# Batch 0 of a fused attention and gated feed-forward kernel: half of k by another queue, six rows per partition, and another unit shape in the first stage

## The chip, the cores and the metric

The kernel runs on one core of one Trainium2 chip. The metric is the device time of one execution in microseconds, as the median of several runs. One execution is also taken with the hardware profiler; its times are those of that one execution. "Span" is the time from its first to its last instruction.

## The reference

Inputs are q, k, v of shape (8 batches, 8 heads, 576 tokens, 64), float32, and two weights, w_in (512 x 2048) and w_out (2048 x 512).

```python
theta = np.pi / 2.0 * pos / S                 # pos = 0..575, S = 576
phi(x) = concat([relu(x) * cos(theta), relu(x) * sin(theta)])     # 64 -> 128 features
kv  = einsum('bhsf,bhsd->bhfd', phi(k), v);   z = phi(k).sum(axis=s)
num = einsum('bhsf,bhfd->bhsd', phi(q), kv);  den = phi(q) . z + 1e-6
x   = (num / den) as (4608 tokens, 512)       # 512 = 8 heads x 64
h   = x @ w_in;   g = h * cos(h);   out = g @ w_out      # (4608, 512) float32
```

Sums over tokens do not depend on the order of the tokens, so the kernel may spread the tokens over the partitions as it likes, as long as the cosine and sine table and the stores follow.

## The kernel before

**Stages.** The 4608 tokens are nine chunks of 512 (`CH`). For each chunk there is a first product M1 (x times w_in), then cosine and product, then a second product M2 (g times w_out). Attention for the eight batches of 576 tokens is woven between these products. Every engine works through its instructions in the order in which the program emits them: `plan` and `at(chunk, step, function, ...)` list what is emitted after which step, and `run(c, s)` emits it. Nothing reorders it afterwards.

**The start, batch 0.** While the inputs travel, TensorE runs products of zeros (`warm`, 33 of them). q is stored with six consecutive tokens on each of 96 partitions (`R = 6`, `PR = 96`); k and v with five consecutive tokens on 112 partitions and four on four more (`RK = 5`, `PK = 116`), so each needs a second small load (`load_rest`). All these loads are issued by GpSimd's queue, which turns float32 into float16 on the way. The queue of SyncE only brings the table `CS`, the identity `ID` and some zeros. `scaled` makes phi: for one token index i it emits two instructions (t = 0 for cosine, t = 1 for sine), each a relu and a product with a column of `CS`. VectorE does most of them; five for k and both for q's i = 4 go to ScalarE. `q_turn` transposes phi(q) of one i on TensorE (eight small products into `QT`), and ScalarE copies `QT` into `X`. `kv_head` sums phi(k) times v over i (five products for each head); ScalarE copies the sums into `kvz`. `num_tile` makes one tile of 128 tokens of the numerators and denominators on TensorE (`NP`) and divides on VectorE (`dn`, `rd`, `x`). `x_turn` transposes it on TensorE (`XP`), and ScalarE, or VectorE for tile 1, copies it into `XT`, from which M1 reads. Tile 0 needs i = 0 and 1, tile 1 needs i = 1 and 2, tile 2 needs i = 2 and 3, and tiles 3 and 4 need i = 4 and 5.

**Chunk 0's M1.** `m1_pair(u, n0, n1)` is a unit: two blocks of 128 columns of w_in by 256 tokens, eight products of 256 columns. Then ScalarE makes the cosine (`co`) and VectorE the product (`g`). Units 0 to 7 go over tiles 0 and 1, units 8 to 15 over tiles 2 and 3. The result of a unit lies in PSUM under the tag `m1` or `m2` by turns, two buffers each, so unit u needs the buffer that unit u-4 has left. `m2_part(0, 0, 0)`, the first of M2, takes such a buffer too. w_in arrives in four groups of four blocks.

**The queue of GpSimd** holds, in this order: k heads 0 to 3, k's rest, k heads 4 to 7, q's i = 0 to 3, v heads 0 and 1, v's rest, v heads 2 to 7 in three loads, w_in group 0, q's i = 4 and 5, w_in groups 1 to 3, w_out groups 0 and 1, then batch 1.

Of the kernel before, what the change touches and what calls it, by code (L numbers as in the profile page):

```python
# [11 lines left out]
ALU = mybir.AluOpType  # L12
# [5 lines left out]
def kernel(  # L18
# [54 lines left out]
    KB = [cpool.tile([PK, H * RUNK], F16, name=f"k{n}") for n in "ab"]  # L73
    VB = [cpool.tile([PK, H * RUNK + D], F16, name=f"v{n}") for n in "ab"]
    ID = cpool.tile([P, P], F16, name="ID")
    WU = cpool.tile([P, CH], F16, name="WU")
    WS = cpool.tile([P, 1], F32, name="WS")
# [14 lines left out]
            q16=lpool.tile([PR, H * RUN], F16, name="q16", tag=f"q16{odd}"),  # L92
        )

    def rows_of(tile_):
        return tile_[:, 0:H * RUNK].rearrange("p (h r) -> p h r", h=H)

    def load_q(b, i0=0, i1=R):
        dst = st[b]["q16"].rearrange("p (h r) -> p h r", h=H)
# [4 lines left out]

    def load_kv(b, which, h0=0, h1=H):
        src = dict(k=k, v=v)[which]
        full = src[b][:, 0:FULL * RK, :].rearrange("h (p i) d -> p h (i d)", i=RK)
        nc.gpsimd.dma_start(  # L108
            out=rows_of(st[b][which + "16"])[0:FULL, h0:h1], in_=full[:, h0:h1],
        )  # L110
# [15 lines left out]

    def scaled(b, which, i, h0=0, h1=H):
        s = st[b]
        rows, n, o = (PR, R, 0) if which == "q" else (PK, RK, R)
        if which + "p" not in s:  # L130
            s[which + "p"] = apool.tile([rows, n, H * F], F16, name=which + "p",
                                        tag=which + "p", bufs=1)
        dst = s[which + "p"][:, i].rearrange("p (h t d) -> p h t d", t=2, d=D)
        src = s[which + "16"][:, 0:H * n * D].rearrange("p (h i d) -> p h i d", i=n, d=D)
        cs = CS[0:rows, :, o + i:o + i + 1]
        for t in range(2):
            if b == 0 and (which == "k" and h0 == 4 and t == 1 or which == "q" and i == 4):
                nc.scalar.activation(
                    out=dst[:, h0:h1, t, :], in_=src[:, h0:h1, i, :], func=AF.Relu,
                    scale=cs[:, t],  # L140
                )
                continue
            nc.vector.tensor_scalar(  # L143
                out=dst[:, h0:h1, t, :], in0=src[:, h0:h1, i, :],
                scalar1=0.0, scalar2=cs[:, t],
                op0=ALU.max, op1=ALU.mult,
            )
# [52 lines left out]
    def kv_head(b, h):  # L200
        s = st[b]
        if h == 0 or (b == 0 and h == 4):
            s["KV"] = psA.tile([P, H, P], F32, name="KV", tag="att")
        if h == 0:
            s["kvz"] = apool.tile([P, H, D + 1], F16, name="kvz", tag="kvz")
        n = P if b == 0 else D + 1
        for i in range(RK):
            if b > 0:
                nc.tensor.matmul(  # L209
                    s["KV"][:, h, 0:n], lhsT=s["kp"][:, i, h * F:(h + 1) * F],  # L210
                    rhs=s["vz"][:, h, i, 0:n], start=(i == 0), stop=(i == RK - 1),
                )
                continue
            base = s["v16"][:, h * RUNK + i * D: h * RUNK + (i + 1) * D]
            vz = bass.AP(
                tensor=base.tensor, offset=base.offset,
                ap=[list(base.ap[0]), [H * RUNK - h * RUNK - i * D, 2], [1, D]],
            )
            nc.tensor.matmul(  # L219
                s["KV"][:, h], lhsT=s["kp"][:, i, h * F:(h + 1) * F], rhs=vz,  # L220
                start=(i == 0), stop=(i == RK - 1),
            )
# [60 lines left out]
    def g_for(c):  # L283
        if ("g", c) not in st:
            st["g", c] = gpool.tile([P, NJT, CH], F16, name="g", tag="g")
        return st["g", c]

    def m1_pair(u, n0, n1):
        j0 = 2 * (u % (NJT // 2))
        M1 = psM.tile([P, 2, CH // 2], F32, name="M1", tag=("m1", "m2")[u % 2])  # L290
        step = P if u == 0 else n1 - n0
        for n in range(n0, n1, step):
            for a in range(2):
                for i in range(NCT):
                    nc.tensor.matmul(  # L295
                        M1[:, a, n - n0:n - n0 + step],
                        lhsT=w_in_sb[:, i, (j0 + a) * P:(j0 + a + 1) * P],
                        rhs=XT[:, i, n:n + step], start=(i == 0), stop=(i == NCT - 1),
                    )
            if u == 0 and n == n0:  # L300
                num_tile(0, 2)
        co = opool.tile([P, 2, CH // 2], F32, name="co", tag="co")
        nc.scalar.activation(out=co, in_=M1, func=AF.Sin, bias=PIH, scale=1.0)  # L303
        nc.vector.tensor_tensor(  # L304
            out=g_for(0)[:, j0:j0 + 2, n0:n1], in0=M1, in1=co, op=ALU.mult,
        )

    def m1_group(c, j):
# [59 lines left out]
    def at(c, s, f, *args):  # L368
        plan.setdefault((c, s), []).append((f, args))
# [10 lines left out]
                load_rest(b, w)  # L380

    def plan_stage0():
        at(0, 0, q_turn, 0, 4)
        at(0, 1, scaled, 0, "q", 5)
        at(0, 1, x_turn, 0, 2)
        at(0, 2, loads, 2, "kvq")
        at(0, 3, q_turn, 0, 5)
        at(0, 4, num_tile, 0, 3)
        at(0, 6, x_turn, 0, 3)
        at(0, 11, num_tile, 0, 4)  # L390
        at(0, 14, x_turn, 0, 4)
# [24 lines left out]
        for i, n in enumerate((-1, 1, 2, 4, 6, 8)):  # L416
            at(0 if n < 0 else 1, z + 15 if n < 0 else n, scaled, 2, "q", i)
            at(0 if n < 0 else 1, z + 15 if n < 0 else n, q_turn, 2, i)
        at(1, 9, loads, 3)
        for h in range(H):  # L420
            at(1, 5 + h // 4, kv_head, 2, h)
# [32 lines left out]
            f(*args)  # L454

    with tc.manual_schedule():
        nc.sync.dma_start(out=CS, in_=cs_dr.ap())
        for n, bufs in enumerate((KB[:1] + VB[:1], KB[1:] + VB[1:])):
            if n:
                nc.sync.dma_start(out=ID, in_=id_dr.ap())  # L460
            for t_ in bufs:
                nc.sync.dma_start(
                    out=rows_of(t_)[FULL:PK, :, REST * D:], in_=zero_dr.ap())
# [3 lines left out]
        tiles_for(0)  # L467
        load_kv(0, "k", 0, 4)
        load_rest(0, "k")
        load_kv(0, "k", 4, 8)  # L470
        load_q(0, 0, 4)
        for h in range(0, H, 2):
            if h == 2:
                load_rest(0, "v")
            load_kv(0, "v", h, h + 2)
        nc.gpsimd.memset(st[0]["v16"][:, H * RUNK:], 1.0)
        load_w_in(0)
        load_q(0, 4, R)
        for g in range(1, 4):
            load_w_in(g)  # L480
        load_w_out(0)
        load_w_out(1)
        loads(1, "kvq")
# [5 lines left out]
            for _ in range(n):  # L489
                nc.tensor.matmul(W, lhsT=WU[:, 0:P], rhs=WU, start=True, stop=True)  # L490

        warm(33)
        for h0 in (0, 4):
            for i in range(RK):
                scaled(0, "k", i, h0, h0 + 4)
        for i in range(4):
            scaled(0, "q", i)
            if i < 2:
                q_turn(0, i)
        for h in range(8):  # L500
            kv_head(0, h)
        q_turn(0, 2, "m2")
        num_tile(0, 0)
# [57 lines left out]
```

## Time and profile before

| what | value |
|---|---|
| median of 3 runs (lowest, highest) | 299.69 us (298.92, 300.45) |
| the profiled execution: its own time | 298.35 us |
| the profiled execution: span | 296.5 us |
| TensorE busy / VectorE / ScalarE / GpSimd | 289.6 / 189.0 / 156.3 / 39.8 us |
| first product of M1 starts (from the span's start) | 18.38 us |
| first product of M2 starts | 35.50 us |
| GpSimd's queue / SyncE's and ScalarE's: bytes | 18.36 MB / 20.08 MB |

The engines are written PE (TensorE), PEld (its weight loads), DVE (VectorE), ACT (ScalarE), POOL (GpSimd) and SP (SyncE). Bytes of a load are counted as they are written, so a float32 input that is turned into float16 counts half of what is read. A line of the timeline has the start, the length, the engine, the line of the program, the operation, what it writes and reads, the shapes, how many instructions were merged, and in brackets the idle time before them with what ended it.

### The profile page before, as it was taken

Reading aid. Unit: us, or ns where it says so; the run is one execution under the profiler, and the core shown is the slowest. Engines: PE = TensorE matmul, PEld = TensorE weight load, DVE = VectorE, ACT = ScalarE, POOL = GpSimd, SP = SyncE. Lnnn points to the kernel's source line nnn. Section 1 sums busy time; section 2 is a strip of 40 time slices with the busy share of each in tenths; the row PEclk is TensorE's granted clock in tenths of the full one; section 3 lists DMA queues with packets and bytes.
Section 4 is the critical chain, followed back from the end, with each engine's and each line's share of the span. In section 5 each row is a group of like instructions: output and inputs, shape, how many; then the busy total and the mean of one; then the engine's idle time right before and its main releaser. Section 6 shows DMA issues by size and latency. Waiting matters only on the chain.

```text
span 296.5 us, 5459 instructions
## 1 busy us (share of the span) xinstructions
PE 289.6 (98%) x2055; PEld 151.7 (51%) x2055; DVE 189.0 (64%) x452; ACT 156.3 (53%) x246; POOL 39.8 (13%) x65
## 2 busy tenths in 40 slices
PE   8899999999999999999999999999999999999994
PEld 3577866554544544455445544554455444444443
DVE  1767888987399666866686768677766267008600
ACT  2587763675357534862477158715771178128511
POOL 8743320005013002100210022000000000000000
PEclk9999999999999999999999999999999999999999
DMA  6999999779999996999799879996802510121022
GB/s 88 182 202 206 199 206 203 182 109 141 172 159 168 159 200 128 196 150 114 130 181 176 149 125 164 149 174 134 167 13 66 123 35 0 38 71 35 2 71 71
DMA packets 78178, 38.83 MB, mean 131 GB/s; under 512 B 48328, under 2 KB 73672, under 8 KB 78152
## 3 DMA queue, kind: packets, MB, share of 16 engines
q0 software_dynamic: 28240, 18.36, 44.7%
q1 hardware_dynamic: 49800, 20.08, 39.8%
q8 instruction: 16, 0.26, 0.4%
q14 instruction: 10, 0.08, 0.1%
q10 hardware_dynamic: 112, 0.05, 0.1%
HBM read 36.76 MB, written 9.44 MB: 156 GB/s over the span
## 4 chain that ended last, share of the span: by engine, by line
PE 92%; DMA 3%; DVE 1%; ACT 1%; POOL 1%; issue 1%; ACTq 0%; POOLq 0%
PE M L342 41%; PE M L311 37%; PE NP L235 4%; PE M L295 3%; PE KV L209 3%; DMA q<-in_q_dram 3%; PE QT L167 1%; PE M L358 1%; PE XP L273 1%; PE KV L219 1%; ACT co L303 1%; DVE qp L143 1%; POOL ka L108 1%; DVE g L304 0%; PE W L490 0%
## 5 line engine op out<-in xcount | busy, mean ns | idle before, releaser
L342 PE MATMUL M<-w_out_sb,g 128*128 128x512 f16 x560 | 128.8, 379 | 0.0
L320 DVE TENSOR_TENSOR g<-M,co 128x512 f16<-128x512 f32 x128 | 87.1, 690 | 54.7 <-ACT co L317 54.7
L311 PE MATMUL M<-XT,w_in_sb 128*128 128x512 f16 x512 | 113.9, 379 | 0.0
L317 ACT ACTIVATE co<-M,PIH 128x512 f32<-128x512 f32 x128 | 88.0, 688 | 26.4 <-PE M L311 26.1
L342 PEld LDWEIGHTS <-g 128*128 128x128 f16 x560 | 52.2, 98 | 56.4
L311 PEld LDWEIGHTS <-w_in_sb 128*128 128x128 f16 x512 | 49.2, 98 | 57.4
L349 ACT ACTIVATE ost<-M 128x512 f32<-128x512 f32 x35 | 20.9, 598 | 90.9 <-PE M L342 76.4
L255 DVE TENSOR_TENSOR x<-NP,rd 128x512 f16<-128x512 f32 x40 | 27.7, 691 | 5.0 <-DMA XT<-x 3.6
L143 DVE TENSOR_SCALAR qp<-q,CS 96x512 f16<-96x512 f16 x94 | 28.5, 350 | 2.4 <-DMA X<-qp 1.4
L143 DVE TENSOR_SCALAR kp<-ka,CS 116x512 f16<-116x512 f16 (+1 forms) x75 | 21.8, 349 | 5.4 <-DMA ka<-in_k_dram 5.4
L235 PEld LDWEIGHTS <-X 128*128 128x128 f16 x320 | 15.3, 98 | 9.3 <-issue 1.2
L100 POOL DMA_DIRECT2D q<-in_q_dram x9 | 7.0, 780 | 90.8 <-DVE qp L143 88.6
L235 PE MATMUL NP<-kvz,X 128*128 128x65 f16 x320 | 17.0, 194 | 0.5 <-issue 0.5
L242 DVE TENSOR_SCALAR dn<-NP 128x8 f32<-128x8 f32 x40 | 6.5, 163 | 15.5 <-PE NP L235 15.1
L295 PE MATMUL M<-XT,w_in_sb 128*128 128x256 f16 (+1 forms) x136 | 15.5, 266 | 0.0
L196 ACT ACTIVATE vz<-va 116x640 f16<-116x640 f16 x20 | 13.5, 728 | 0.0
L304 DVE TENSOR_TENSOR g<-M,co 128x512 f16<-128x512 f32 x16 | 10.8, 688 | 3.6 <-ACT co L303 3.5
L295 PEld LDWEIGHTS <-w_in_sb 128*128 128x128 f16 x136 | 12.3, 98 | 1.3
L303 ACT ACTIVATE co<-M,PIH 128x512 f32<-128x512 f32 x16 | 11.0, 688 | 3.3 <-PE M L295 2.9
L490 PE MATMUL W<-WU 128*128 128x512 f16 x39 | 11.5, 452 | 1.2 <-DVE PIH L465 1.2
L209 PEld LDWEIGHTS <-kp 116*128 116x128 f16 x280 | 10.8, 97 | 3.1
L209 PE MATMUL KV<-vz,kp 116*128 116x65 f16 x280 | 11.3, 193 | 0.0
(42 smaller groups left out, 106.0 us busy)
## 6 DMA issues: line engine op xcount, KB each, us to landing
out_dram<-ost SPq DMA_DIRECT2D x23, 192.0 KB, 2.4
q<-in_q_dram POOLq DMA_DIRECT2D x7, 576.0 KB, 7.5
ka<-in_k_dram POOLq DMA_DIRECT2D x6, 560.0 KB, 14.8
va<-in_v_dram POOLq DMA_DIRECT2D x6, 560.0 KB, 12.1
out_dram<-ost SPq DMA_DIRECT2D x24, 128.0 KB, 5.8
w_in_sb<-in_moe_w_in_dram POOLq DMA_DIRECT2D x4, 512.0 KB, 10.1
w_out_sb<-in_moe_w_out_dram POOLq DMA_DIRECT2D x4, 512.0 KB, 16.5
out_dram<-ost SPq DMA_DIRECT2D x23, 64.0 KB, 2.5
```

The lines of the kernel that those rows point to most:

```text
L143: nc.vector.tensor_scalar(out=dst[:, h0:h1, t, :], in0=src[:, h0:h1, i, :], scalar1=0.0, scalar2=cs[:, t], op0=ALU.max, op1=ALU.mult,)
L196: nc.scalar.activation(out=dst, in_=src[:, h:h + 2], func=AF.Copy)
L209: nc.tensor.matmul(s["KV"][:, h, 0:n], lhsT=s["kp"][:, i, h * F:(h + 1) * F], rhs=s["vz"][:, h, i, 0:n], start=(i == 0), stop=(i == RK - 1),)
L235: nc.tensor.matmul(NP[:, h // 4, o:o + D + 1], lhsT=s["X"][:, h, c0:c0 + P], rhs=s["kvz"][:, h], start=True, stop=True,)
L255: nc.vector.tensor_tensor(out=x4[:, a0:a1], in0=np4[:, a0:a1, :, 0:D], in1=rd[:, a0:a1].broadcast_to((P, a1 - a0, 4, D)), op=ALU.mult,)
L295: nc.tensor.matmul(M1[:, a, n - n0:n - n0 + step], lhsT=w_in_sb[:, i, (j0 + a) * P:(j0 + a + 1) * P], rhs=XT[:, i, n:n + step], start=(i = ...
L303: nc.scalar.activation(out=co, in_=M1, func=AF.Sin, bias=PIH, scale=1.0)
L311: nc.tensor.matmul(M1, lhsT=w_in_sb[:, i, j * P:(j + 1) * P], rhs=XT[:, i, c * CH:(c + 1) * CH], start=(i == 0), stop=(i == NCT - 1),)
L317: nc.scalar.activation(out=co, in_=M1, func=AF.Sin, bias=PIH, scale=1.0,)
L320: nc.vector.tensor_tensor(out=g_for(c)[:, j], in0=M1, in1=co, op=ALU.mult,)
L342: nc.tensor.matmul(M2, lhsT=st["g", c][:, j, m * P:(m + 1) * P], rhs=w_out_sb[:, j], start=(j == 0), stop=(j == NJT - 1),)
L349: nc.scalar.activation(out=ost, in_=M2, func=AF.Copy)
```

## The change

Five things change, all in batch 0 and chunk 0.

1. **k and v of batch 0** lie on 96 partitions with six tokens each, like q. The two rest loads go; `kv_head` sums over six products of 96 rows for each head instead of five of 116.
2. **k heads 0 to 3** are loaded as float32 into a tile `k32` by SyncE's queue, as its first load. `CS` and `ID` go to ScalarE's queue. GpSimd's queue starts with k heads 4 to 7.
3. **`scaled` for k**: 24 instructions instead of 20. ScalarE has the sine of all six i of heads 0 to 3 and of i = 0 to 2 of heads 4 to 7; VectorE has the other 15. For q's i = 4 both go to VectorE, for i = 5 the sine to ScalarE.
4. **Order on TensorE at the start**: 29 products of zeros instead of 33; `q_turn` 0 and 1 stand before heads 0 and 2 of `kv_head`.
5. **Units**: `m1_unit(u, j0, nj, t0)`. Four pairs over tiles 0 and 1, then two units of four blocks by the 128 tokens of tile 2, then four pairs, two units of tile 2, and four units of tile 3. q's i = 4 and 5 are loaded behind w_in group 1, and the steps at which their scaling and turning, tiles 3 and 4 and their turns are emitted change.

```diff
 def load_kv(b, which, h0=0, h1=H):
+    if b == 0:
+        nc.gpsimd.dma_start(
+            out=rows_of(st[b][which + "16"], RUN)[0:PR, h0:h1],
+            in_=src[b].rearrange("h (p i) d -> p h (i d)", i=R)[:, h0:h1],
+        )
+        return
...
 def scaled(b, which, i, h0=0, h1=H):
+        if b == 0 and which == "k" and h0 == 0:
+            src = s["k32"].rearrange("p (h i d) -> p h i d", i=n, d=D)
...
-            if b == 0 and (which == "k" and h0 == 4 and t == 1 or which == "q" and i == 4):
+            if b == 0 and t == 1 and (
+                    which == "k" and (h0 == 0 or i < 3) or which == "q" and i == 5):
                 nc.scalar.activation(
...
 def kv_head(b, h):
-        for i in range(RK):
+        for i in range(RK if b > 0 else R):
...
-    def m1_pair(u, n0, n1):
-        j0 = 2 * (u % (NJT // 2))
-        M1 = psM.tile([P, 2, CH // 2], F32, name="M1", tag=("m1", "m2")[u % 2])
-        step = P if u == 0 else n1 - n0
+    def m1_unit(u, j0, nj, t0):
+        nt = 4 // nj
+        n0 = t0 * P
+        M1 = psM.tile([P, nj, nt * P], F32, name="M1", tag=("m1", "m2")[u % 2])
+        step = P if u == 0 else nt * P
...
     def plan_stage0():
-        at(0, 0, q_turn, 0, 4)
-        at(0, 1, scaled, 0, "q", 5)
         at(0, 1, x_turn, 0, 2)
         at(0, 2, loads, 2, "kvq")
-        at(0, 3, q_turn, 0, 5)
-        at(0, 4, num_tile, 0, 3)
-        at(0, 6, x_turn, 0, 3)
-        at(0, 11, num_tile, 0, 4)
-        at(0, 14, x_turn, 0, 4)
+        at(0, 3, scaled, 0, "q", 4)
+        at(0, 4, q_turn, 0, 4)
+        at(0, 4, scaled, 0, "q", 5)
+        at(0, 5, q_turn, 0, 5)
+        at(0, 7, num_tile, 0, 3)
+        at(0, 10, x_turn, 0, 3)
+        at(0, 12, num_tile, 0, 4)
+        at(0, 15, x_turn, 0, 4)
...
-        nc.sync.dma_start(out=CS, in_=cs_dr.ap())
...
+        st[0]["k32"] = gpool.tile([PR, H // 2 * RUN], F32, name="k32", tag="g")
+        nc.sync.dma_start(
+            out=st[0]["k32"].rearrange("p (h r) -> p h r", r=RUN),
+            in_=k[0].rearrange("h (p i) d -> p h (i d)", i=R)[:, 0:H // 2],
+        )
+        nc.scalar.dma_start(out=CS, in_=cs_dr.ap())
+        nc.scalar.dma_start(out=ID, in_=id_dr.ap())
...
-        load_kv(0, "k", 0, 4)
-        load_rest(0, "k")
         load_kv(0, "k", 4, 8)
         load_q(0, 0, 4)
         for h in range(0, H, 2):
-            if h == 2:
-                load_rest(0, "v")
             load_kv(0, "v", h, h + 2)
...
         load_w_in(0)
+        load_w_in(1)
         load_q(0, 4, R)
...
-        warm(33)
+        warm(29)
...
         for i in range(4):
             scaled(0, "q", i)
-            if i < 2:
-                q_turn(0, i)
         for h in range(8):
+            if h in (0, 2):
+                q_turn(0, h // 2)
             kv_head(0, h)
...
-        scaled(0, "q", 4)
         x_turn(0, 1)
-        for s in range(NJT):
-            n = s // (NJT // 2) * (CH // 2)
-            m1_pair(s, n, n + CH // 2)
+        units = [(2 * p, 2, 0) for p in range(4)] + [(0, 4, 2), (4, 4, 2)]
+        units += [(2 * p, 2, 0) for p in range(4, 8)] + [(8, 4, 2), (12, 4, 2)]
+        units += [(4 * g, 4, 3) for g in range(4)]
+        for s, (j0, nj, t0) in enumerate(units):
+            m1_unit(s, j0, nj, t0)
             run(0, s)
```

More of the change, by code (lines that the diff above doesn't have):

```diff
@@ L72 @@
     CS = cpool.tile([PK, 2, R + RK], F32, name="CS")
-    KB = [cpool.tile([PK, H * RUNK], F16, name=f"k{n}") for n in "ab"]
-    VB = [cpool.tile([PK, H * RUNK + D], F16, name=f"v{n}") for n in "ab"]
+    KB = [cpool.tile([PK, H * w], F16, name=f"k{n}") for n, w in (("a", RUN), ("b", RUNK))]
+    VB = [cpool.tile([PK, H * w + D], F16, name=f"v{n}") for n, w in (("a", RUN), ("b", RUNK))]
     ID = cpool.tile([P, P], F16, name="ID")
@@ L93, in tiles_for, with rows_of @@
         )
-    def rows_of(tile_):
-        return tile_[:, 0:H * RUNK].rearrange("p (h r) -> p h r", h=H)
+    def rows_of(tile_, run=RUNK):
+        return tile_[:, 0:H * run].rearrange("p (h r) -> p h r", h=H)
     def load_q(b, i0=0, i1=R):
@@ L128, in scaled @@
         s = st[b]
-        rows, n, o = (PR, R, 0) if which == "q" else (PK, RK, R)
+        rows, n, o = (PR, R, 0) if which == "q" or b == 0 else (PK, RK, R)
         if which + "p" not in s:
-            s[which + "p"] = apool.tile([rows, n, H * F], F16, name=which + "p",
+            s[which + "p"] = apool.tile([PR if which == "q" else PK, R, H * F], F16, name=which + "p",
                                         tag=which + "p", bufs=1)
-        dst = s[which + "p"][:, i].rearrange("p (h t d) -> p h t d", t=2, d=D)
-        src = s[which + "16"][:, 0:H * n * D].rearrange("p (h i d) -> p h i d", i=n, d=D)
+        dst = s[which + "p"][0:rows, i].rearrange("p (h t d) -> p h t d", t=2, d=D)
+        if b == 0 and which == "k" and h0 == 0:
+            src = s["k32"].rearrange("p (h i d) -> p h i d", i=n, d=D)
+        else:
+            src = s[which + "16"][0:rows, 0:H * n * D].rearrange(
+                "p (h i d) -> p h i d", i=n, d=D)
         cs = CS[0:rows, :, o + i:o + i + 1]
         for t in range(2):
-            if b == 0 and (which == "k" and h0 == 4 and t == 1 or which == "q" and i == 4):
+            if b == 0 and t == 1 and (
+                    which == "k" and (h0 == 0 or i < 3) or which == "q" and i == 5):
                 nc.scalar.activation(
@@ L213, in kv_head @@
                 continue
-            base = s["v16"][:, h * RUNK + i * D: h * RUNK + (i + 1) * D]
+            base = s["v16"][0:PR, h * RUN + i * D: h * RUN + (i + 1) * D]
             vz = bass.AP(
                 tensor=base.tensor, offset=base.offset,
-                ap=[list(base.ap[0]), [H * RUNK - h * RUNK - i * D, 2], [1, D]],
+                ap=[list(base.ap[0]), [H * RUN - h * RUN - i * D, 2], [1, D]],
             )
             nc.tensor.matmul(
-                s["KV"][:, h], lhsT=s["kp"][:, i, h * F:(h + 1) * F], rhs=vz,
-                start=(i == 0), stop=(i == RK - 1),
+                s["KV"][:, h], lhsT=s["kp"][0:PR, i, h * F:(h + 1) * F], rhs=vz,
+                start=(i == 0), stop=(i == R - 1),
             )
@@ L286, in g_for @@
         return st["g", c]
-    def m1_pair(u, n0, n1):
-        j0 = 2 * (u % (NJT // 2))
-        M1 = psM.tile([P, 2, CH // 2], F32, name="M1", tag=("m1", "m2")[u % 2])
-        step = P if u == 0 else n1 - n0
-        for n in range(n0, n1, step):
-            for a in range(2):
+    def m1_unit(u, j0, nj, t0):
[3 more added lines that the diff above has]
+        step = P if u == 0 else nt * P
+        for n in range(0, nt * P, step):
+            for a in range(nj):
                 for i in range(NCT):
                     nc.tensor.matmul(
-                        M1[:, a, n - n0:n - n0 + step],
+                        M1[:, a, n:n + step],
                         lhsT=w_in_sb[:, i, (j0 + a) * P:(j0 + a + 1) * P],
-                        rhs=XT[:, i, n:n + step], start=(i == 0), stop=(i == NCT - 1),
+                        rhs=XT[:, i, n0 + n:n0 + n + step],
+                        start=(i == 0), stop=(i == NCT - 1),
                     )
-            if u == 0 and n == n0:
+            if u == 0 and n == 0:
                 num_tile(0, 2)
-        co = opool.tile([P, 2, CH // 2], F32, name="co", tag="co")
+        co = opool.tile([P, nj, nt * P], F32, name="co", tag="co")
         nc.scalar.activation(out=co, in_=M1, func=AF.Sin, bias=PIH, scale=1.0)
         nc.vector.tensor_tensor(
-            out=g_for(0)[:, j0:j0 + 2, n0:n1], in0=M1, in1=co, op=ALU.mult,
+            out=g_for(0)[:, j0:j0 + nj, n0:n0 + nt * P], in0=M1, in1=co, op=ALU.mult,
         )
@@ L456 @@
     with tc.manual_schedule():
-        nc.sync.dma_start(out=CS, in_=cs_dr.ap())
[L458 to L463, printed above, removed]
+        tiles_for(0)
+        st[0]["k32"] = gpool.tile([PR, H // 2 * RUN], F32, name="k32", tag="g")
[5 more added lines that the diff above has]
+        nc.scalar.dma_start(out=ID, in_=id_dr.ap())
+        for t_ in KB + VB:
+            nc.sync.dma_start(
+                out=rows_of(t_)[FULL:PK, :, REST * D:], in_=zero_dr.ap())
         nc.vector.memset(WU, 0.0)
@@ L466 @@
         nc.scalar.activation(out=WS, in_=PIH, func=AF.Sin)
-        tiles_for(0)
-        load_kv(0, "k", 0, 4)
-        load_rest(0, "k")
         load_kv(0, "k", 4, 8)
@@ L472 @@
         for h in range(0, H, 2):
-            if h == 2:
-                load_rest(0, "v")
             load_kv(0, "v", h, h + 2)
-        nc.gpsimd.memset(st[0]["v16"][:, H * RUNK:], 1.0)
+        nc.gpsimd.memset(st[0]["v16"][0:PR, H * RUN:], 1.0)
         load_w_in(0)
+        load_w_in(1)
         load_q(0, 4, R)
-        for g in range(1, 4):
-            load_w_in(g)
+        load_w_in(2)
+        load_w_in(3)
         load_w_out(0)
@@ L490, in warm @@
                 nc.tensor.matmul(W, lhsT=WU[:, 0:P], rhs=WU, start=True, stop=True)
-        warm(33)
+        warm(29)
         for h0 in (0, 4):
-            for i in range(RK):
+            for i in range(R):
                 scaled(0, "k", i, h0, h0 + 4)
```

## The prediction

> **What bounds the kernel now.** I read the page's busy times and chain first, then the chain in order of time, the DMA issues, the stretches of half a microsecond, and the timeline of the first 37 us.
>
> ```profile
> PE 289.6 (98%) x2055; PEld 151.7 (51%) x2055; DVE 189.0 (64%) x452; ACT 156.3 (53%) x246; POOL 39.8 (13%) x65
> PEclk9999999999999999999999999999999999999999
> PE 92%; DMA 3%; DVE 1%; ACT 1%; POOL 1%; issue 1%; ACTq 0%; POOLq 0%
> ```
>
> PE carries the end: 92% of the chain. Behind the first M1 product (18.38 us) it hardly rests, so what moves PE's first M2 product moves the end one for one. Two quantities decide: when M1 starts, and how long PE needs from there to M2 (35.50, so 17.12 us).
>
> ```profile
> 3.46 7.46 DMA q<-in_q_dram
> 10.92 0.02 issue
> 10.94 1.38 DVE qp L143 x4
> ...
> 12.88 2.23 PE KV L219 x40
> 15.12 0.34 PE QT L167 x8
> ```
>
> The chain in time says what sets the start: q lands at 10.92, DVE scales it, PE turns it, sums KV, turns i = 2, and a fixed string of ACT, DVE and PE steps leads from there to M1.
>
> ```profile
> ka<-in_k_dram POOLq DMA_DIRECT2D x2, 280.0 KB, 5.3
> ...
> q<-in_q_dram POOLq DMA_DIRECT2D x1, 384.0 KB, 7.5
> ...
> ID<-id_const SPq DMA_DIRECT2D x1, 32.0 KB, 4.0
> ```
>
> These are loads, KB as written and us from issue to landing. The stretches show who moves bytes when (last column GB/s):
>
> ```profile
> 1.50:2.00 0.50, 0.50 (x2) 0.15 (x1) 0.00 (x0) 0.50 (x1) 0.50 (x1) 1.00 0.15 18
> 2.00:2.50 0.50, 0.50 (x3) 0.20 (x2) 0.00 (x0) 0.22 (x2) 0.50 (x2) 1.00 0.02 3
> 2.50:3.00 0.50, 0.50 (x3) 0.22 (x2) 0.00 (x0) 0.00 (x0) 0.50 (x2) 1.00 0.30 33
> 4.00:4.50 0.50, 0.50 (x2) 0.15 (x1) 0.00 (x0) 0.00 (x0) 0.50 (x2) 1.00 1.35 200
> ```
>
> SP's first load, issued at 0.74, moves bytes from about 1.6; POOL's first, issued at 1.31, from about 2.8. From 4 us to q's landing the stretches hold 116 to 200 GB/s, 155 in the mean.
>
> The timeline shows what a scaling of q costs PE when it is emitted late (i = 5):
>
> ```profile
> 20.80 0.39 PE L273 MATMUL XP<-ID,x 128*128 128x128 f16 x4
> 21.00 0.69 ACT L303 ACTIVATE co<-M,PIH 128x512 f32<-128x512 f32 x1
> ...
> 21.73 0.69 DVE L304 TENSOR_TENSOR g<-M,co 128x512 f16<-128x512 f32 x1 [0.59 <-ACT co L303]
> ...
> 22.33 0.60 DVE L143 TENSOR_SCALAR qp<-q,CS 96x512 f16<-96x512 f16 x2
> ...
> 22.99 0.51 PE L167 MATMUL QT<-ID,qp 96*128 96x96 f16 x8
> ...
> 23.56 0.80 ACT L186 ACTIVATE X<-QT 128x768 f16<-128x768 f16 x1
> ```
>
> Unit 1 leaves PE at 20.80. Its cosine runs 0.20 later, its g at +0.93, the two scalings behind that g at +1.53, and the turn starts at +2.19. PE had a turn of x (0.22) and two units (0.87 each) to do meanwhile, and still idled 0.22.
>
> **The start, part by part.** Bytes ahead of q's landing: before 280 + 16 + 280 + 384 = 960 KB in POOL's queue; after 288 (as float16; the same float32 reads) by SP, 288 + 384 by POOL: the same 960. If both queues share the same engines, q gains the time by which SP's first bytes are earlier, 1.2 us, and little for dropping the 16 KB rest: q lands at 9.6. Bounds: SP's half costs POOL's queue nothing, 304 KB less at 155 GB/s, 1.9 us, q at 9.0; or SP's lead is lost, q at 10.8. I take 9.6, since CS's row shows the lead. The Trainium skill says it the same way ("DMA: Bandwidth & Descriptors", section "Issuing engines are not separate DMA queues"): queues of several engines interleave on the same 16, so a second one saves only issue time; strictly by it, with no earlier bytes, q would land at 10.8 and the sum below would be 1.2 us more; the trace's earlier SP bytes speak for a part between.
>
> DVE must be through k by 9.6. k's half in SP's queue: 0.74 + 5.3 (POOL's row) less 0.5 for the faster first byte, so about 5.4; the bounds are 4.6 (bytes from 1.6, 288 KB at 200 GB/s, and the 1.6 us by which q's landing trails the stretch in which 960 KB are through) and 6.5 (first rival). Six scalings from float32: no row has that source; the float16 row (15 in 3.38) gives 0.225 each and is one end, the float32 rate of L255 and L242 (0.69 for 512 elements, 0.16 for 8, so 0.42 for 256) the other; 0.30 taken, nearer the same operation: 7.2. The second half of k lands about 1.2 us ahead of the 8.4 at which ACT could start on it, at 7.2; nine scalings at 0.225 end at 9.3. ACT has nine in place of five (five in 2.10, 0.42 each): 5.4 + 2.5, then 1.3: 9.2. Both are just covered by q's 9.6; each us beyond costs a us. CS and ID cost ACT two issues (0.34 and 0.45 on SP) while it has nothing due; CS had moved within 1.3 us of its issue and is wanted at 5.4: nothing. The zero loads, now behind k's half, serve batches 1 and 2 only: nothing.
>
> From q: turn 0 starts 0.67 later as before (10.94 to 11.61); turn 0.34, twelve KV products at 0.056 (40 in 2.23) 0.67, turn 0.34, thirty-six more 2.01: turn 2 at q + 4.03. Before it was 14.95 - 10.94 = 4.01: the eight extra products (0.45) take the place of PE's waits for i = 1. v's last load trails q by its 576 KB as before and is needed 3.4 us after q: covered by 0.2. The zeros end four products (0.86 us) earlier, at 9.9, ahead of turn 0 at 10.3: nothing. From turn 2 to M1 nothing changes, and w_in group 0 (landed by 17.10, where a POOL load had waited for it) comes 1.3 us earlier too, ahead of M1. So M1 starts 1.3 us earlier: **-1.3**, between -1.9 and about 0.
>
> **M1 to M2, walked from M1's first product at 0.** PE's work: a pair is 8 x 0.109 (40 in 4.37) = 0.874; a unit of four blocks is 16 x 0.0558 = 0.893, as the unit in steps of 128 has shown; a turn of q 0.345, of x 0.22, an NP 0.26. Before, 16.14 of work and 0.98 idle make 17.12. After, eight units at +0.019 give 16.29. The idle time:
> - XP2: x2 is ready at 2.09, PE at 2.03: 0.07. (Turn 4 stood there before.)
> - Turn 4: its two scalings now stand behind unit 3's g, and only unit 4 lies between. Unit 3 ends at 4.06; the turn can start 2.19 later, 6.25; PE is through unit 4 at 4.96: **1.30**.
> - Turn 5: ACT's sine for i = 5 is emitted behind turn 4's copy X, which starts 0.57 after the turn, at 6.82; ACT is free 0.69 later and needs 0.71: 8.27. PE has turn 4 until 6.60 and unit 5 until 7.49: **0.78**.
> - Unit 12 reads tile 3: unit 10 ends at 13.26, co10 runs from 13.46, XT3 behind it from 14.04 for 0.60, so 14.72; PE is through unit 11 at 14.38: 0.34.
> - M2 takes unit 13's buffer; that g stands behind tile 4's three DVE steps: 0.14.
>
> Idle 2.63, stage 18.92: **+1.80**. Tiles 3 and 4's other waits (0.20 and 0.51 before) are covered now: two pairs lie before NP3, three units before XP3. w_in group 1, which had landed by 20.69, comes 1.3 us earlier and no longer behind q's 192 KB; unit 2 wants it at 19.4: covered. q's end lands one w_in (2.5 us) later and 1.3 earlier, about 19.2; DVE wants it at 22.7. If it came after that, turn 4 would wait longer by as much.
>
> **Sum.** -1.3 + 1.8 = +0.5 us: the profiled execution's 298.35 (span 296.5 and 1.85 around it) becomes 298.85. It lies 1.34 below the median, so the median becomes 299.69 + 0.5 = 300.2. A measurement of this kernel can tell about 0.5%, 1.5 us, from no change: the forecast is no change, because a start that is won is given back by two turns of q.
>
> **Rivals.**
> *SP's load comes late (slower).* ID, 32 KB in SP's queue beside POOL's loads, took 4.0 us. With that latency and 1.8 us for its bytes k's half lands at 6.5; six scalings at 0.30 and nine at 0.225 end at 10.3, or 11.1 with 0.42 each. M1 then gains 0.6 or nothing: 300.9 to 301.6; with the lead lost for q too (10.8), 301.4. It decides once k's half lands after 5.8. For it: POOL's own first half took 5.3. Against: SP issues 0.6 us before POOL, on idle engines.
> *PE's clock falls (slower).* PE idles 2.1 of the 4.6 us from unit 3's end to unit 6. The first twelve zeros ran at half speed (0.43 against 0.216) for 5.0 us; one such stretch costs 2.5 us: 302.7. Against it: the clock row is whole throughout and the idle 0.74 us before turn 0 left it so. The Trainium skill ("TensorE: Matmul & The Clock Gate", section "HAM oscillation — how this bites in real kernels") forbids only gaps over about 3.4 us; by it this rival does not happen.
> *The turns do not wait (faster).* If q's scalings reach DVE ahead of g3, the 2.08 us of the two turns go: 298.1. Against it: before, L143's pair ran exactly behind the g that it was emitted after.
>
> **How the numbers follow.** Forecast 0.64: slower by over 0.5% 0.05, faster 0.02, the rest within. Late or lost lead 0.22: 0.15 slower, 0.07 within. Clock 0.06, all slower. No waits 0.08: 0.06 faster, 0.02 within. Together 0.08 faster, 0.66 same, 0.26 slower. The forecast alone spans 299.6 (q at 9.0) to 301.2; the range 298.7 to 302.3 leaves out most of the no-wait case, the clock case and the far end of the late load.
>
> **What would show it.** q's first scaling at 9.6 and M1 at 17.1 (start); turn 4 idle 1.3 behind DVE's qp, turn 5 idle 0.8 behind ACT's qp, unit 12 idle 0.3 behind ACT's XT; M1 to M2 in 18.9. It is wrong if M1 starts later than 17.8 or before 16.4, if PE does not stop at the turns, or if the clock row shows less than 9.

## The result, and the profile after

| what | before | after |
|---|---|---|
| median of 21 runs (lowest, highest) | 298.25 us (297.38, 300.45) | 299.48 us (298.37, 302.85) |
| ratio after / before, 95% interval | | 1.0045 (1.0029 to 1.0060) |
| the profiled execution: time, span | 298.35, 296.5 us | 299.29, 297.5 us |
| q's first scaling starts | 10.94 us | 10.04 us |
| first product of M1 starts | 18.38 us | 17.50 us |
| first product of M2 starts | 35.50 us | 36.40 us |
| from M1's first product to M2's | 17.12 us | 18.90 us |
| from the start of PE's last product to the end of the span | 4.00 us | 4.51 us |

The change makes the kernel slower by a little less than half a per cent. With more runs the median of before came to 298.25, 1.44 below the three runs that the prediction started from; the predicted 300.2 lies 0.7 above the measured 299.48, and its difference of +0.5 us stands against a measured +1.2.

On the page after the change, PE is as busy as before, the row of the granted clock is whole, and PE still carries 93% of the chain:

```profile
PE 289.4 (97%) x2123; PEld 153.0 (51%) x2123; DVE 189.6 (64%) x453; ACT 157.4 (53%) x249; POOL 37.9 (13%) x62
PEclk9999999999999999999999999999999999999999
PE 93%; DMA 3%; DVE 1%; ACT 1%; issue 1%; POOL 0%; ACTq 0%; POOLq 0%
```

The chain of waits over the first 60 us (start, length, what) shows both halves of the change. q is scaled 0.90 earlier than before, and KV now runs as twelve products behind the first turn and thirty-six behind the second. Later two scalings of q (DVE at 23.19, ACT at 25.02) and a copy into XT (ACT at 31.57) stand in the chain. Before, the chain ran through ACT and DVE there too (a scaling of q at 22.42, tile 3's division until 26.88), but PE idled for them only 0.2 to 0.5 us at a time:

```profile
2.12 7.90 DMA q<-in_q_dram
10.04 0.62 DVE qp L154 x2
10.71 0.51 PE QT L178 x8
...
12.23 2.01 PE KV L230 x36
...
23.19 0.53 DVE qp L154 x2
...
25.02 0.72 ACT qp L149
...
31.57 0.60 ACT XT L292
```

The timeline shows the two turns. The bracket is the idle time before an instruction and what ended it: PE's weight loader waits 1.30 us for DVE's scaling of i = 4 and 0.78 us for ACT's sine of i = 5. The scaling starts where g of unit 3 (22.50 + 0.69) releases DVE, and the sine where ACT's copy X has started and ACT is free again:

```profile
22.50 0.69 DVE L317 TENSOR_TENSOR g<-M,co 128x512 f16<-128x512 f32 x1 [0.18 <-ACT co L316]
...
23.76 0.37 PEld L178 LDWEIGHTS <-qp 96*128 96x128 f16 x8 [1.30 <-DVE qp L154]
...
24.31 0.81 ACT L197 ACTIVATE X<-QT 128x768 f16<-128x768 f16 x1 [0.96 <-PE QT L178]
...
25.02 0.71 ACT L149 ACTIVATE qp<-q,CS 96x512 f16<-96x512 f16 x1
...
25.78 0.37 PEld L178 LDWEIGHTS <-qp 96*128 96x128 f16 x8 [0.78 <-ACT qp L149]
```

The loads of the start (KB as written, us from issue to landing):

```profile
k<-in_k_dram SPq DMA_DIRECT2D x1, 576.0 KB, 5.0
q<-in_q_dram POOLq DMA_DIRECT2D x1, 384.0 KB, 7.9
ka<-in_k_dram POOLq DMA_DIRECT2D x1, 288.0 KB, 6.2
```

SP's half of k was issued at 0.74 and landed at about 5.7. The stretches show its bytes early, as the prediction had it (last column GB/s; before, the first two held 18 and 3):

```profile
1.50:2.00 0.50, 0.50 (x2) 0.15 (x1) 0.00 (x0) 0.34 (x1) 0.50 (x1) 1.00 0.51 75
2.00:2.50 0.50, 0.50 (x3) 0.20 (x2) 0.00 (x0) 0.50 (x1) 0.50 (x2) 1.00 0.62 167
```

Between the two profiled executions the end moved by +0.96 us: the start -0.88, the stage from M1 to M2 +1.78, waits between M2 and the last product -0.45, and the time after the last product (here and below counted from its start) +0.51. The prediction has the first two; the last two are new.

### The profile page after: what moved, and what is told of

It is laid out like the page before. It is cut to its first block, busy times and chain, and to the rows that moved or that the text cites. A ratio compares the mean times of both kernels' runs of the same rounds, so it can differ in the third digit from the quotient of the medians.

```text
span 297.5 us, 5599 instructions
## 1 busy us (share of the span) xinstructions
PE 289.4 (97%) x2123; PEld 153.0 (51%) x2123; DVE 189.6 (64%) x453; ACT 157.4 (53%) x249; POOL 37.9 (13%) x62
## 4 chain that ended last, share of the span: by engine, by line
PE 93%; DMA 3%; DVE 1%; ACT 1%; issue 1%; POOL 0%; ACTq 0%; POOLq 0%
PE M L355 41%; PE M L324 37%; PE M L307 4%; PE NP L246 4%; PE KV L220 3%; DMA q<-in_q_dram 3%; PE QT L178 1%; PE M L371 1%; PE KV L230 1%; PE XP L284 1%; DVE x L266 0%; DVE qp L154 0%; ACT co L316 0%; POOL ka L108 0%; ACT qp L149 0%
## 5 line engine op out<-in xcount | busy, mean ns | idle before, releaser
L324 PEld LDWEIGHTS <-w_in_sb 128*128 128x128 f16 x512 | 49.3, 98 | 57.3
L154 DVE TENSOR_SCALAR kp<-ka,CS 116x512 f16<-116x512 f16 (+1 forms) x69 | 20.0, 339 | 0.0
L307 PE MATMUL M<-XT,w_in_sb 128*128 128x128 f16 (+1 forms) x200 | 15.6, 234 | 0.1
L307 PEld LDWEIGHTS <-w_in_sb 128*128 128x128 f16 x200 | 13.6, 98 | 0.9 <-issue 0.3
L317 DVE TENSOR_TENSOR g<-M,co 128x512 f16<-128x512 f32 x16 | 10.8, 688 | 4.7 <-ACT co L316 4.6
L504 PE MATMUL W<-WU 128*128 128x512 f16 x35 | 10.8, 469 | 1.2 <-DVE PIH L483 1.2
```

Source lines behind the costliest of these rows:

```text
L154: nc.vector.tensor_scalar(out=dst[:, h0:h1, t, :], in0=src[:, h0:h1, i, :], scalar1=0.0, scalar2=cs[:, t], op0=ALU.max, op1=ALU.mult,)
L307: nc.tensor.matmul(M1[:, a, n:n + step], lhsT=w_in_sb[:, i, (j0 + a) * P:(j0 + a + 1) * P], rhs=XT[:, i, n0 + n:n0 + n + step], start=(i = ...
L324: nc.tensor.matmul(M1, lhsT=w_in_sb[:, i, j * P:(j + 1) * P], rhs=XT[:, i, c * CH:(c + 1) * CH], start=(i == 0), stop=(i == NCT - 1),)
```

## The experiments

Every profile is one execution, and the executions of one kernel differ: the four with the old start (before, the stage alone, and two below) have M1 at 18.38, 18.16, 18.64 and 19.11. So I use the times of twelve executions as well as the profiles, and for M1, the stage and the end the means over the profiles of one kind. Ratios are to the kernel before on the same chip.

### The scalings of q two units earlier

```diff
-        at(0, 3, scaled, 0, "q", 4)
-        at(0, 4, scaled, 0, "q", 5)
+        at(0, 1, scaled, 0, "q", 4)
+        at(0, 2, scaled, 0, "q", 5)
```

> The changed kernel with one edit: the scalings of q's i = 4 and 5 are emitted after units 1 and 2 instead of 3 and 4; the turns stay where they are. Theory (PE waits at the two turns because the scalings stand behind unit 3's g and behind turn 4's copy): both waits (1.13 to 1.30 and 0.61 to 0.78 us) go, M1 to M2 takes 16.8 us instead of 18.9, the span falls by 2.1 us to about 295.4, ratio to the kernel before 0.996. Rival (the four-block units bind by themselves, ACT and DVE fall behind, and the idle time only moves on): M1 to M2 stays above 18.3, ratio 1.003 to 1.005.

Ratio 0.9994 (0.9968 to 1.0019). In its profile both waits at the turns are gone: M1 17.50, M2 34.32, 16.81 between them, as expected. That shows that the turns' idle time comes from where the scalings are emitted. The expected time, ratio 0.996, lies just outside the interval: against the change's 1.0045, about 1.5 of the 2.08 us came through at the end (0.0051 of 298.4), with some 0.9 us of doubt from the two intervals.

### The start alone, the stage alone

The first is the changed kernel with the old units, plan and order of q; the second is the kernel before with `m1_unit`, the new units, the new plan, q's end behind w_in group 1 and the new engines for scaling q's i = 4 and 5.

> The changed kernel's start (k and v on 96 rows, half of k by SyncE's queue, 29 products of zeros, the new order of turns and heads) with the units, the plan, q's load order and the engines for q's i = 4 and 5 of the kernel before. Theory (the two parts add up): M1 starts at 17.5 as in the changed kernel, M1 to M2 takes 17.1 as before, M2 starts at 34.6, 0.9 us before the kernel before: ratio 0.997. Rival (the early start is lost again in the stage, since w_in or q's end is late for it): M2 at 35.3 or later, ratio 0.999 to 1.001.

> The kernel before with only the stage of the changed one: the units, the plan, q's end behind w_in group 1, and VectorE and ScalarE as changed for q's i = 4 and 5. Theory: M1 starts at 18.4 as before, M1 to M2 takes 18.9, M2 starts 1.8 us later than before: ratio 1.006. Rival (q's end, 1.0 us later here than in the changed kernel, holds the scaling of i = 4): 2.2 us or more, ratio 1.008.

Stage alone: ratio 1.0060 (1.0033 to 1.0087), M1 18.16 to M2 37.30, idle at the turns 1.54 and 0.78. The stage is 0.23 longer than in the changed kernel's profile, since the first scaling took that much longer; otherwise this is as expected. Start alone: ratio 1.0015 (0.9984 to 1.0046). M1 at 17.37 and M2 at 34.66 are as expected, the time is not: in the profile 5.67 us lie between PE's last product and the end, and the ratio leaves out the expected 0.997.

### k of batch 0 by GpSimd's queue alone

The edit, shortened; `scaled` then reads heads 0 to 3 as float16 too:

```diff
-        nc.sync.dma_start(out=st[0]["k32"]..., in_=k[0]...[:, 0:H // 2])
+        load_kv(0, "k", 0, 4)
         load_kv(0, "k", 4, 8)
```

> The changed kernel with heads 0 to 3 of k loaded as float16 by GpSimd's queue, first in it, instead of as float32 by SyncE's. Theory (SyncE's queue moves its bytes while GpSimd's has none under way): q lands at about 10.8 instead of 10.0, M1 starts 0.8 us later, ratio to the kernel before 1.006 to 1.008 (changed kernel 1.0045). Rival (the same 16 engines move the same reads, so who issues doesn't matter): q lands at 10.0 to 10.2, ratio 1.004 to 1.005.

Ratio 1.0063 (1.0041 to 1.0086). The start went the other way than I expected. q is scaled at 9.68 and M1 starts at 17.14, both 0.36 earlier than with SP's load. In its DMA issues:

```profile
ka<-in_k_dram POOLq DMA_DIRECT2D x2, 288.0 KB, 4.8
q<-in_q_dram POOLq DMA_DIRECT2D x1, 384.0 KB, 6.9
```

SP's float32 half is not what brings q forward. What this kernel still has of the change is the row layout, 96 rows of six tokens in place of 112 of five, and with it the 16 KB rest load is gone. Before, q's load stood behind three issues (0.84, 0.62 and 0.71 us) and was issued at 3.46, 7.46 us before it landed; here it stands behind two (1.48 us), is issued at 2.78 and lands 6.9 us later. The table by ACT's queue is no part of the gain: the kernel before with that alone scales q at 11.68, and this start with the table by SP scales it at 10.06.

The trace speaks more for the layout than for the issue that is gone. GpSimd's first bytes move at 2.84 us here and at 2.86 before, and from 4 us on the DMA engines are busy nine tenths of the time or more in nearly every slice of both profiles. But from 4 us to q's landing they move 189 GB/s here, and 181 in the second profile with this start (in the last section), against 159 to 165 in the four with the old start. A packet of k or v, six tokens of 64 float16 numbers, holds 768 B and takes 84 ns in the mean; with five tokens it holds 640 B and takes 76. No run has the new layout and the rest load together, so how the gain splits between them is not shown.

The kernel's time is not shorter for it. Its profile has a wait of 1.94 us near 108 us, which the chain calls "issue" and in which DVE's row waits for X<-qp:

```profile
108.18 1.94 issue
110.12 0.42 PE NP L243 x8
```

### Loads of chunk 4 emitted later

In nearly every profile PE waits at that place, for tile 3 of batch 3: DVE waits there for a transposing load X<-qp in SP's queue, issued at 95 to 100 us and landed 10 us or more later, while GpSimd's loads of batch 4 are under way. After the first four experiments I took this for the place where a gain is swallowed, and emitted those loads six steps later.

```diff
-            at(c, 4, loads, c + 2)
+            at(c, 10 if c == 2 else 4, loads, c + 2)
```

> The kernel before with one edit: batch 4's loads are emitted after step 10 of chunk 2 instead of step 4 (about 5 us later). Theory (at 108 us PE waits for the transposes of batch 3's phi(q) in SyncE's queue, which crawl beside these loads; it waited 0.68 us in the kernel before): the transposes land before 104, the wait goes, the last M2 product comes 0.7 us earlier, ratio 0.9977. Rival (the engines have so many bytes to move by then that the wait only changes its place, to batch 4's v and k): ratio 1.000 or more, with a new PE wait behind 109 us.

> The changed kernel with the same edit. Theory: its own wait at 108 was 0.30 us; the last M2 product comes 0.15 us later than in the kernel before, ratio 1.0005. What separates it from the kernel before with that edit is then the whole 0.83 to 0.90 us by which its M2 starts later. Rival (the edit only shifts the wait): ratio 1.0045 or more.

> The changed kernel with the scalings of q's i = 4 and 5 emitted after units 1 and 2 and batch 4's loads after step 10 of chunk 2. Theory: M2 starts at 34.3 and the 1.25 us by which it is ahead at the end of chunk 1 are no longer lost at 108 us, where the kernel before loses 0.68: the last M2 product comes 1.9 us earlier than in the kernel before, ratio 0.9935. Rival (a bound by bytes): PE waits again between 108 and 115 us and the last product comes at the time of the kernel before, ratio 0.999 to 1.000.

Ratios 1.0014 (0.9985 to 1.0043), 1.0049 (1.0023 to 1.0074) and 0.9970 (0.9943 to 0.9996). None of the intervals holds the expected ratio (0.9977, 1.0005, 0.9935). DVE's wait at that place is 0.23 us in the third kernel's profile, and 2.18 us in the second's, which has the same edit:

```profile
106.53 0.61 DVE L154 TENSOR_SCALAR qp<-q,CS 96x512 f16<-96x512 f16 x2 [0.23 <-DMA X<-qp]
```

```profile
111.55 0.61 DVE L154 TENSOR_SCALAR qp<-q,CS 96x512 f16<-96x512 f16 x2 [2.18 <-DMA X<-qp]
```

The edit does not do what it was made for: it moves no load. GpSimd issues batch 4's q at nearly the same point in the kernel before and with the edit, when DVE's scalings release it, and not at a step of PE's work:

```profile
88.06 0.78 POOL L100 DMA_DIRECT2D q<-in_q_dram  x1 [17.30 <-DVE qp L143]
```

```profile
88.94 0.78 POOL L100 DMA_DIRECT2D q<-in_q_dram  x1 [17.54 <-DVE qp L143]
```

Counted from chunk 2's first M2 product, that is 12.7 us and 12.4 us ahead, not the 5 us later that I had written. The transposing load issued at 95 to 100 us takes 10.1 to 12.9 us to land in all thirteen profiles with PE at its rate, edit or not. So the theory about these loads stays untested, and the three kernels are in effect second measurements of the kernel before, of the change and of the earlier scalings. As such they are of use: the earlier scalings gain 0.0079 on the change here (2.4 us) where the first pair gave 0.0051 (1.5 us), in the mean nearly the 2.08 us of the two turns.

M2's start alone does not decide the wait: the stretch from M2's first product to PE's last varies from 256.3 to 258.9 us over all profiles with PE at its rate, and is 257.7 in the mean for the six that start M2 before 35 us and 257.3 for the seven others. The wait differs from execution to execution; that it swallows what is won early is not shown.

The second kernel's profile shows one more thing, the rival that I had given 0.06. The idle at the turns is the same 1.30 and 0.78, but from 25.6 us, just behind the second idle piece, PE's granted clock (third column from the end) halves for 3.4 us, and M1 to M2 takes 20.55 us:

```profile
24.00:26.00 2.00, 1.39 (x24) 1.22 (x22) 0.31 (x2) 1.94 (x3) 0.78 (x1) 0.90 1.25 207
26.00:28.00 2.00, 2.00 (x14) 1.46 (x12) 0.69 (x1) 0.86 (x2) 0.63 (x1) 0.50 1.28 210
28.00:30.00 2.00, 2.00 (x22) 1.59 (x20) 0.69 (x1) 1.21 (x2) 0.12 (x1) 0.75 1.34 197
```

### All steps forward

On top of the third kernel of the last section:

```diff
-        at(0, 4, q_turn, 0, 4)
-        at(0, 5, q_turn, 0, 5)
-        at(0, 7, num_tile, 0, 3)
-        at(0, 10, x_turn, 0, 3)
-        at(0, 12, num_tile, 0, 4)
+        at(0, 3, q_turn, 0, 4)
+        at(0, 4, q_turn, 0, 5)
+        at(0, 6, num_tile, 0, 3)
+        at(0, 9, x_turn, 0, 3)
+        at(0, 11, num_tile, 0, 4)
```

> The same with turns 4 and 5 after units 3 and 4, tile 3 after unit 6, its turn after unit 9, tile 4 after unit 11. Theory: the waits for tile 3's copy (0.31) and for unit 13's buffer (0.14) go, about 0.15 idle comes in front of turn 4: M1 to M2 16.5 us, M2 at 34.0, the last M2 product 2.2 us earlier than in the kernel before, ratio 0.9925. Rival as in the run above: 0.999.

Ratio 0.9983 (0.9958 to 1.0008). M1 17.32 to M2 33.83, so 16.51, as walked; of the 1.67 us by which M2 is earlier, 1.31 reach the end of the profiled execution, but only 0.5 the ratio; the expected 0.9925 is missed.

### The end of the span

All seven profiles with the new start so far have 4.51 to 5.67 us between PE's last product and the end, all three with the old one 4.00 to 4.03. In the longer ones a packet of queue 14, "instruction", runs 1.5 to 2.3 us after the last product, among the last stores; in the others it runs 5 us after, when all is stored. The change had moved the loads of CS and ID from SP's queue to ACT's, which changes how many instructions each engine has. Of the next four runs the first makes this move in the kernel before, and the others undo it.

```diff
-        nc.scalar.dma_start(out=CS, in_=cs_dr.ap())
-        nc.scalar.dma_start(out=ID, in_=id_dr.ap())
+        nc.sync.dma_start(out=CS, in_=cs_dr.ap())
+        nc.sync.dma_start(out=ID, in_=id_dr.ap())
```

> The kernel before with one difference: the table CS and the identity are loaded by ScalarE's queue and not by SyncE's. All seven profiles with the new start have 4.51 to 5.67 us between PE's last product and the end of the span, all three with the old start 4.00 to 4.03; in the longer ones an instruction fetch falls on a DMA engine just when the last stores land. Theory (the length of ScalarE's and SyncE's instruction streams moves where that fetch falls): with these two issues moved the tail becomes 4.5 or more, and the kernel 0.5 us slower, ratio about 1.002; start and M1 to M2 as before (M1 18.4, M2 35.5). Rival (the new start's longer streams on other engines, or its data, make the tail): the tail stays 4.0 and the ratio 1.000.

> The changed kernel with CS and the identity back in SyncE's queue, behind k's float32 half. Theory of the instruction fetch: the tail goes from 4.51 back to 4.0, the end 0.5 us earlier, ratio about 1.003 (changed kernel 1.0045). Rival (something else in the new start): the tail stays 4.5. On the start: CS now stands behind 576 KB in its own queue; if it lands before 5.8, when k's half is there anyway, nothing moves and M1 stays at 17.5; if it lands later, the six float32 scalings wait, and M1 comes later by that where DVE was not covered.

> The best of the parts so far: k of batch 0 wholly by GpSimd's queue as float16 (six tokens on 96 rows), CS and the identity in SyncE's queue, q's i = 4 and 5 scaled behind units 1 and 2, chunk 4's loads issued six steps later. The POOL-only start gave M1 at 17.14 and the early scaling a stage of 16.8, so M2 at 33.9 to 34.0, 1.5 us earlier than before; with late loads no wait near 108 us. Theory of the instruction fetch: tail 4.0, the end 1.5 us earlier, ratio 0.995. Rival: tail 4.6, end 0.9 earlier, ratio 0.997; if a wait near 108 us remains as in the kernel with all steps moved, up to 0.5 us less again.

> The kernel with all steps moved forward (scalings behind units 1 and 2, turns at steps 3 and 4, late loads), now with CS and the identity back in SyncE's queue. Theory of the instruction fetch: it comes some 4.4 us after PE's last product and the tail is 4.0 to 4.1, not 4.5. Means over the profiles so far give start -1.1, stage -0.7, tail 0: 1.8 us earlier than before, ratio 0.994, or 0.997 in an execution with a wait near 108 us. Rival (the earlier fetch belongs to the new start itself): tail 4.5 or more, ratio 0.996 to 0.998.

The kernel before with the table by ACT: ratio 0.9996 (0.9972 to 1.0020), end 4.03, the fetch at 4.53 in place of 5.03: it came earlier by half a microsecond, not by enough to meet the stores. That expectation missed. The changed kernel with the table by SP: ratio 1.0044 (1.0019 to 1.0069). Its profiled execution took 615.95 us because TensorE ran at half its rate from beginning to end, so nothing is read from its end; at the start the scaling of k waited for CS until 5.3 us and was still through 0.27 us before q landed, so CS delayed nothing. GpSimd's start with early scalings: ratio 0.9984 (0.9963 to 1.0005), fetch at 4.41, end 4.10. All steps forward with the table by SP: ratio 0.9965 (0.9935 to 0.9994), fetch at 4.36, end 4.05. The last and the earlier scalings with late loads (0.9970) are the only two whose interval lies below 1, by very little, and the same kernel without the late loads, an edit that moved nothing, had 0.9994.

The DMA view of the last microseconds in the kernel before (one digit for each eighth of a microsecond from 293 us; the end is at 296.54, and the lone 2 behind it is the fetch):

```profile
DMA  0059107799975200000000000000000000002000
```

The same view after the change (one digit for each eighth of a microsecond from 293 us; the end is at 297.50):

```profile
DMA  0000027513797996330000000000000000000000
...
q14 instruction: 1, 0.01, 0.5%
...
out_dram<-ost SPq DMA_DIRECT2D x1, 16.0 KB, 2.5
```

And of the last kernel (from 291 us; the end is at 295.64):

```profile
DMA  9581000000393047997862000000000000000002
...
q14 instruction: 1, 0.01, 0.7%
...
out_dram<-ost SPq DMA_DIRECT2D x1, 16.0 KB, 1.9
```

After the change no packet stands by itself: the fetch runs among the stores, and the last 16 KB need 2.5 us. In the last kernel the fetch is the lone 2 at the far end, and the same store needs 1.9. With the new start and the table by ACT the end is 4.51 us or more in seven profiles of seven, with the new start and the table by SP 4.05 and 4.10, with the old start 4.00 to 4.03 in four. Which engine's instructions are fetched there, and why start and table are both needed, stays open.

The times of twelve executions do not show this term. I had expected the changed kernel with the table by SP to come down to about 1.003; it has 1.0044 against 1.0045. All steps forward came down from 0.9983 to 0.9965, within the intervals, and GpSimd's start with early scalings (0.9984, expected 0.995) lies no lower than SP's start with them and the table by ACT (0.9994 and 0.9970). So the longer end is seen in the profiles alone.

## Why the prediction was right and wrong

**The stage: right in every term.** Predicted 18.92, measured 18.90. Turn 4 idles 1.30 (1.30 predicted), turn 5 0.78 (0.78), unit 12 0.31 (0.34), M2 0.14 (0.14). The walk held because every step came from an order in the program and a duration in the trace. (Its sums for turn 5 and for unit 12 hold 0.05 and 0.08 us more than the durations named there; the trace shows 0.04 between an engine's end and the start of the one that waits for it.) The rival in which the turns do not wait is out, and the first experiment shows that they would not if the scalings were emitted two units earlier.

**The start: direction right, reason wrong.** Predicted -1.3, profiled -0.88; the means over seven profiles with SP's load (17.48) and four with the old start (18.57) give -1.09. The terms: SP's half landed at 5.7 for 5.4; six scalings from float32 took 2.06, 0.34 each for 0.30; the nine behind them ended at 9.74 for 9.3, and q landed at 10.02 for 9.6, so k was just covered. The step that failed is the one that gave the whole gain to SP's earlier bytes and "little" to the 16 KB rest load. Without SP's load M1 starts at 17.14 and 17.52 in two profiles, no later than with it (17.25 to 17.92 in seven). The Trainium skill's sentence ("DMA: Bandwidth & Descriptors", section "Issuing engines are not separate DMA queues"), that a second queue saves issue time alone, is borne out by this; what I had drawn from it, q at 10.8 without SP's lead, is not, since q is scaled at 9.68 there. The prediction counted equal bytes ahead of q as equal time; with the new rows the DMA engines moved 181 to 189 GB/s in place of 159 to 165, and one issue of 0.62 us had gone. The split between the two is not shown.

**"What moves PE's first M2 product moves the end one for one": it holds for the stage and not for the start.** In the profiles the end has a term of its own, +0.5 to +0.6, which the sum lacked and which came with the change though no store was touched. And PE waits later for loads. The sum of the means, against the measured ratios times 298.4, in us:

| kernel | start | M1 to M2 | end | sum | measured (interval) |
|---|---|---|---|---|---|
| the change | -1.09 | +1.62 | +0.64 | +1.17 | +1.34 (+0.87 to +1.79) |
| scalings earlier | -1.09 | -0.55 | +0.64 | -1.00 | -0.18 (-0.95 to +0.57) |
| start alone | -1.09 | 0 | +0.64 | -0.45 | +0.45 (-0.48 to +1.37) |
| stage alone | 0 | +1.62 | 0 | +1.62 | +1.79 (+0.98 to +2.60) |
| k by GpSimd | -1.24 | +1.62 | +0.64 | +1.02 | +1.88 (+1.22 to +2.57) |
| before, late loads | 0 | 0 | 0 | 0 | +0.42 (-0.45 to +1.28) |
| change, late loads | -1.09 | +1.62 | +0.64 | +1.17 | +1.46 (+0.69 to +2.21) |
| scalings earlier, late loads | -1.09 | -0.55 | +0.64 | -1.00 | -0.90 (-1.70 to -0.12) |
| all steps forward | -1.09 | -0.85 | +0.64 | -1.30 | -0.51 (-1.25 to +0.24) |
| before, table by ACT | 0 | 0 | 0 | 0 | -0.12 (-0.84 to +0.60) |
| change, table by SP | -1.09 | +1.62 | +0.06 | +0.59 | +1.31 (+0.57 to +2.06) |
| GpSimd's start, earlier, table by SP | -1.24 | -0.55 | +0.06 | -1.73 | -0.48 (-1.10 to +0.15) |
| all forward, table by SP | -1.09 | -0.85 | +0.06 | -1.88 | -1.04 (-1.94 to -0.18) |

(Start: M1 17.48 or 17.33 against 18.57. Stage: 18.98 in three profiles with the new units, 16.81 and 16.51 with earlier scalings, against 17.36 in four with the old ones. End: 4.66, the middle of seven, or 4.08, against 4.02.) The change itself comes near, +1.17 for +1.34, but the sums as a whole do not hold. The ten kernels with the new start lie on average 0.67 above them, the three with the old one 0.16, and the start alone has the other sign. Nor is the term of the end borne out: the three kernels with the table by SP, whose sums have almost none of it, lie 0.94 above, the seven with the table by ACT 0.56.

A simpler reading fits the times better. Leave out start and end and count the stage alone: then the ten kernels with the new start lie on average 0.02 above it, the three with the old one 0.16. So in these times the stage counts one for one, and of the 1.1 to 1.2 us by which the new start is earlier nothing is seen at the end. That reading was made after the fact, and a single kernel's interval reaches 0.5 to 0.9 us to either side.

Where the start's gain goes is seen in part. With the all-forward kernel and the table by SP, M2 is 1.49 earlier than before, the next chunk's M2 0.75, since PE there waits for batch 1's v: the load vb landed at 36.3 us, and GpSimd, which issued two more loads before it filled `vz`, was through at 39.1. GpSimd's start lost 0.60 in the same chunk. The other place is the wait near 108 us: from chunk 2's first M2 product to chunk 3's it takes 30.2 us at the shortest, 0.6 more in the mean of four profiles with the old start (0 to 1.2) and 1.2 more in nine with the new one (0 to 2.1). Whether an earlier start makes these waits longer, a spread of this size doesn't settle.

**The clock.** The rival priced at 2.5 us exists: in one profiled execution the clock halved behind the two idle pieces at the turns, and the stage took 1.65 us longer (20.55 against 18.90). The same pieces left the clock whole in the profiles of the change, of the stage alone and of k by GpSimd, so this does not make the median. Nor is a fall of the clock bound to these pieces: six of 116 executions of the kernel before had a mean granted clock of 0.991 to 0.994 too, and took 300.3 to 301.1 us. Seven of 68 with the turns' waits had it. Why it fell is not shown. The Trainium skill ("TensorE: Matmul & The Clock Gate", section "HAM oscillation — how this bites in real kernels") warns of idle gaps over about 3.4 us; here none was that long, and the measurement decides.

**The late load of SP** did not happen: 5.7 us is just inside the 5.8 from which it would have decided.

It was luck that the number came so near. Two errors of opposite sign did it: the sum was 0.7 us short, and the median that it was put on was 1.44 too high. As a difference the forecast was +0.5, inside what a measurement can tell from none; the true one, +1.2 to +1.3, lies just below that bound. What the sum lacked is, in the reading above, the loss of the start's gain on its way to the end.

## What to carry to other kernels

Walk an in-order stage instruction by instruction from the trace: where a scaling is emitted behind the wrong product, the stall could be foretold here to a few hundredths of a microsecond in one profile and to a quarter of one in another, and it went when the scaling was emitted two units earlier. Don't carry a gain at the start unchanged to the end: ask which later waits end with a load and not with the engine that carries the chain, and compare several profiles, since one execution's start moved by half a microsecond with no change in it. When an edit is to move a load, look in the trace whether the load moved: emitted six steps later, it was issued where it had been. And before a second queue is given the credit for a load that lands earlier, run the same rows through the old queue; here longer rows and one small load less brought q as early, and the second queue added nothing.

## What the runs showed of the hardware

- In seven profiles a packet of the instruction queue (8 KB) ran beside the last stores, 1.5 to 2.3 us after the start of the last product, and the end came 4.51 to 5.67 us after it. In the six with that packet at 4.4 us or later the end came at 4.00 to 4.10. With the new start it depended on which queue two small loads at the very start stood in; with the old one it did not. The times of twelve executions do not show the difference.
- While GpSimd's queue brought k, q and v, the DMA engines moved 181 and 189 GB/s with packets of 768 B for k and v (84 ns each) and 159 to 165 with packets of 640 B (76 ns), and were busy in both.
- The transposing load X<-qp issued by SP's queue at 95 to 100 us took 10.1 to 12.9 us to land, while GpSimd's loads were under way; the wait for it varied from 0.2 to 2.6 us on DVE.
- A scaling of 96 x 256 elements from float32 took 0.34 us in the mean of six on DVE, against 0.21 from float16 for the nine behind them.
- TensorE's granted clock halved for 3.4 us behind idle pieces of 1.30 and 0.78 us in one profile, and not in three others with such pieces. One execution ran at about half rate throughout (large products 682 ns in place of 379), with a mean granted clock of 1.000 on record.
